# The last ten jobs of a cross network reordered, and the small tails batched to match

## The chip, the cores and the metric

The kernel runs on one core of one Trainium2 chip. The time is the device time of one execution in microseconds (us), as the median of three runs. Engines are named as the profile names them: PE is TensorE (matrix multiply), PEld its weight loads, ACT is ScalarE, DVE is VectorE, POOL is GpSimd, and SP is SyncE, which here only issues DMAs.

## The reference

A cross network of a recommender: six layers over 16384 rows of 416 features, everything in bfloat16.

```python
B, F, D, L = 16384, 26, 16, 6
Din = min(F * D, 1024)            # 416
# x0: (B, Din), ws: (L, Din, Din), bs: (L, Din)
x = x0
for l in range(L):
    proj = jnp.einsum('bd,de->be', x, ws[l]) + bs[l]
    x = x0 * proj + x
return x
```

## The kernel before, in words

**Tiles.** The rows are cut into eight groups of 2048 (four chunks of 512). Activations are held transposed: features on the 128 partitions, rows along the free axis. 416 features are three full tiles of 128 and a remainder of 32, called the tail; the tails of a group's four chunks lie side by side in the four quarters of one 128 x 512 tile. A **job** (g, l) is layer l of group g, so there are 48 jobs. A job is three output tiles of 128 features and its tail.

**One tile.** `full` (L467) issues 12 matmuls of 128x128 weights against 512 columns (three input tiles, four chunks), into four of the eight PSUM banks; `rows32` (L486) adds the contribution of the 32 tail features, with four 32-row matmuls that run side by side. `evacuate` (L378) empties the banks: ScalarE adds the bias (L406), two banks in one instruction where they are neighbours and one otherwise, VectorE multiplies by x0 (L415) and adds the old x (L420). Switching between full and 32-row matmuls is kept rare by pairing tiles: the first of a pair does full matmuls and then its rows ("FR"), the second its rows and then the full ones ("RF"). A tile without a partner ahead of a tails batch is "F1": its rows are sixteen 32x32 matmuls (L494). An FR tile's banks are all finished at its end, by the rows; an RF tile's first bank is finished when nine of the twelve full matmuls are done.

**Tails.** `tails` (L506) does the 32-feature outputs of several jobs together: 32x32 matmuls (L512), then 128x32 ones (L521), one bank for each job; `evacuate_tail` (L427) does bias (L446), multiply (L448), add (L450). For groups whose index isn't a multiple of four, the add reads a copy rotated by 32-partition steps, which two small DMAs write (`prefill` and `rotate`, L337 and L338).

**Order.** `order` (L217) lists the 48 jobs by hand: a diagonal sweep in which the jobs between two layers of one group belong to other groups. The second half mirrors the first, and L221 replaces the last six. `cuts` (L223) cuts the list into the batches of tails. `where` (L745) places each batch behind tile 0 of its second job; the last batch is placed behind tile 0 of (6, 5). L756 to 758 move tiles 1 and 2 of job (7, 4) to the end of the list. A pass behind it shifts a batch by one tile where an odd number of tiles would not stand ahead of it, and another (L797) gives each tile its mode; the last item is always "RF". The banks come from a ring of eight: four for each tile, one for each tail of a batch. The instructions are emitted in this order on each engine; a small planner derives the semaphore waits from reads and writes, and no engine's queue is reordered, SP's neither.

**When a job is done** (`done_with`, L363: three tiles and the tail) its input buffers are freed, the next rotated tail is started, and after layer 5 `output` (L687) queues on SP: DMA transposes of the three tiles into `ost` (L691) and of the tails into `ot` (L699), a copy of the tails into place (`spread`: POOL L720, for group 6 ScalarE L718), and the store (L727). For group 6 the stores are issued only ahead of the last job.

**The last job**, (7, 5), is written out by hand (from L863): it swaps the operands, so its output comes out in the layout of the result (L876: 128 rows x 416 features), and needs no transposing afterwards. For its residual, the input x of that job has to be turned into that layout: input tiles 0 and 1 by DMA (`rest_turn` L733, issue L739: tile 0 in one transpose, tile 1 in two halves), which are issued behind tiles 0 and 1 of job (7, 4); input tile 2 on TensorE (L887) and VectorE (L896); the tail on TensorE (L901) and ScalarE (L909). It starts with matmuls on input tiles 0 and 1, chunk by chunk (`nat_full`), so it needs the outputs of tiles 0 and 1 of (7, 4) at once. Each of its four rounds is then 12 matmuls of L876 with rows (L917) and bias (L922), four copies out of PSUM (L928), two multiplies (L934), two adds (L940) and a store (L947); the last round's are finer.

Of the kernel before, what the change touches and what calls it, by code (L numbers as in the profile page):

```python
# [198 lines left out]
def bass_standalone__cross_network_dcn__recsys_kernel(  # L199
# [7 lines left out]
    L = ws.shape[0]  # L207
    NT = 3
# [5 lines left out]
    LAST = NG - 1  # L214
    NX0, NXS, NX3, NTW, NTS = 5, 6, 10, 4, 4

    order = [(0, 0), (0, 1), (1, 0), (0, 2), (1, 1), (2, 0), (0, 3), (1, 2), (2, 1), (3, 0),  # L217
             (0, 4), (1, 3), (2, 2), (3, 1), (0, 5), (1, 4), (2, 3), (3, 2), (4, 0), (1, 5),
             (2, 4), (3, 3), (4, 1), (5, 0)]
    order += [(NG - 1 - g, L - 1 - l) for g, l in reversed(order)]  # L220
    order[-6:] = [(5, 5), (7, 3), (6, 4), (7, 4), (6, 5), (7, 5)]  # L221
    assert len(set(order)) == NG * L
    cuts = [1, 2, 3, 4, 4, 4, 4, 4, 4, 4, 4, 4, 3, 2]  # L223
    batches = []
    n = 0
    for c in cuts:
# [515 lines left out]
                writes=[("x5n", j, t) for j in range(j0, j1)], lane=f"x5_{t}{j0}", batch=0)  # L742

    items = []
    where = {(b[min(1, len(b) - 1)], 0): b for b in batches[:-1]}  # L745
    where[((LAST - 1, L - 1), 0)] = batches[-1]
    del where[((0, 0), 0)]
    where[((0, 1), 0)] = where.pop(((1, 0), 0))
    tiles = [((1, 0), 0), ((1, 0), 1), ((0, 1), 0), ((0, 1), 1), ((0, 1), 2), ((1, 0), 2)]
# [1 line left out]
    for jb, i in tiles:  # L751
        items.append(("tile", jb, i))
        if (jb, i) in where:
            items.append(("tails", where[(jb, i)]))

    for i in range(1, NT):  # L756
        late = items.index(("tile", (LAST, L - 2), i))
        items.append(items.pop(late))


    single = 0
# [263 lines left out]
```

## Time and profile before

| | |
|---|---|
| median of three runs | 475.86 us (475.6 to 476.08) |
| profiled execution, span | 474.40 us; its own device time is not listed, and the median less the span is 1.46 us |
| PE busy | 463.0 us of the span |
| DVE / ACT busy | 404.5 / 341.2 us |
| full matmuls L479 | 1701 recorded, 372.1 us |
| output | 13.63 MB written |

A profile line names engine, source line, operation, output<-inputs, and how many instructions are merged; a timeline line begins with start and length in us. A note in brackets tells how long the engine had been idle and for what. "SPq" lines are the issue of DMAs on SP; their data moves later. Matmul starts are recorded and their ends are modelled, so the distance between two starts is the better measure of TensorE's pace.

### The profile page before, as it was taken

The numbers are of one execution on the slowest core, as the hardware profiler recorded it, in microseconds if no ns is written. First come the engines' busy times: TensorE is split into PE (matmuls) and PEld (weight loads), VectorE is DVE, ScalarE is ACT, GpSimd is POOL, SyncE is SP. The second block draws the span as 40 slices with busy tenths as digits, with TensorE's granted clock in tenths as the row PEclk, the third lists the DMA queues.
The fourth block names the chain that finished last, engine by engine and source line by source line (L and its number), as shares of the span: only waits on it lengthen the run. The fifth ranks groups of instructions, "written<-read, shape, count | busy, mean of one in ns | idle before, by whom it ended". The sixth has DMA issues, their size and how long they took to land.

```text
span 474.4 us, 8414 instructions
## 1 busy us (share of the span) xinstructions
PE 463.0 (98%) x3354; PEld 200.0 (42%) x3408; DVE 404.5 (85%) x700; ACT 341.2 (72%) x371; POOL 6.6 (1%) x15
## 2 busy tenths in 40 slices
PE   8999999999999999999999999999999999999996
PEld 5344444654444444444444444444444444444442
DVE  1888888888888888898889869988888888888897
ACT  4687777777777777777777777777777777777775
POOL 1000000000000000000000000000000000001000
PEclk9999999999999999999999999999999999999999
DMA  8996830730102388369319950880001039026999
GB/s 224 183 176 142 177 84 1 137 87 1 33 2 46 69 234 145 76 146 233 89 24 163 245 102 7 191 271 1 1 10 27 0 62 240 22 46 102 234 166 289
DMA packets 139052, 53.18 MB, mean 112 GB/s; under 512 B 112763, under 2 KB 138501, under 8 KB 139013
## 3 DMA queue, kind: packets, MB, share of 16 engines
q1 hardware_dynamic: 138856, 52.54, 50.0%
q8 instruction: 26, 0.43, 0.4%
q10 hardware_dynamic: 156, 0.11, 0.1%
q14 instruction: 14, 0.11, 0.1%
HBM read 5.97 MB, written 13.63 MB: 41 GB/s over the span
## 4 chain that ended last, share of the span: by engine, by line
PE 92%; DMA 2%; DVE 2%; ACT 2%; issue 1%; SPq 0%; DVEq 0%
PE ps L479 77%; PE ps L500 7%; PE ps L521 6%; ACT tw L406 2%; DMA wm<-in_ws_dram 1%; PE ps L494 1%; DVE x L940 1%; DMA x<-x 1%; DVE x L934 1%; PE ps L512 1%; DMA ot<-x 1%; DVE tw L415 0%; PE ps L600 0%; SPq L545 0%; DVE x L610 0%
## 5 line engine op out<-in xcount | busy, mean ns | idle before, releaser
L406 ACT ACTIVATE tw<-ps,bias 128x1024 bf16<-128x1024 f32 (+1 forms) x295 | 299.8, 1071 | 119.5 <-PE ps L500 81.1
L479 PE MATMUL ps<-x,wm 128*128 128x512 bf16 (+1 forms) x1701 | 372.1, 371 | 6.2 <-issue 3.7
L479 PEld LDWEIGHTS ps<-x,wm 128*128 128x128 bf16 x1755 | 165.1, 98 | 209.5 <-issue 28.2
L415 DVE TENSOR_TENSOR tw<-tw,x 128x1024 bf16<-128x1024 bf16 (+1 forms) x285 | 192.6, 683 | 51.9 <-ACT tw L406 51.5
L420 DVE TENSOR_TENSOR x<-tw,x 128x1024 bf16<-128x1024 bf16 (+1 forms) x285 | 182.5, 681 | 0.0
L500 PE MATMUL ps<-x,w 32*128 32x512 bf16 x512 | 39.2, 379 | 0.0
L521 PE MATMUL ps<-x,wm 128*32 128x512 bf16 x564 | 33.0, 380 | 0.0
L446 ACT ACTIVATE ts<-ps,bias 128x512 bf16<-128x512 f32 x47 | 28.8, 701 | 0.0
L450 DVE TENSOR_TENSOR x<-ts,x 128x512 bf16<-128x512 bf16 x47 | 18.6, 417 | 3.9 <-DMA x<-x 3.9
L521 PEld LDWEIGHTS ps<-x,wm 128*32 128x32 bf16 x564 | 13.8, 96 | 17.6 <-issue 5.3
L500 PEld LDWEIGHTS ps<-x,w 32*128 32x128 bf16 x512 | 7.8, 92 | 26.9 <-issue 26.4
L448 DVE TENSOR_TENSOR ts<-ts,x 128x512 bf16<-128x512 bf16 x47 | 18.6, 418 | 0.0
L720 POOL COPY ost<-ot 128x512 bf16<-128x512 bf16 x6 | 5.1, 854 | 422.2 <-DMA ot<-x 422.2
L876 PE MATMUL ps<-wm,x 128*128 128x416 bf16 x48 | 9.7, 340 | 0.0
L610 DVE COPY x<-ps 128x512 bf16<-128x512 bf16 x5 | 2.0, 423 | 8.9 <-PE ps L600 8.9
L928 ACT ACTIVATE x<-ps 128x416 bf16<-128x416 f32 x16 | 7.7, 517 | 2.1 <-PE ps L876 1.9
L612 ACT ACTIVATE x<-ps 128x512 bf16<-128x512 bf16 x7 | 3.8, 595 | 5.6 <-PE ps L600 5.6
L876 PEld LDWEIGHTS ps<-wm,x 128*128 128x128 bf16 x48 | 4.2, 98 | 4.4 <-issue 1.0
L512 PE MATMUL ps<-x,w 32*32 32x512 bf16 x188 | 5.9, 374 | 0.0
L494 PE MATMUL ps<-x,w 32*32 32x512 bf16 x208 | 5.6, 385 | 0.0
L940 DVE TENSOR_TENSOR x<-x,x 128x832 bf16<-128x832 bf16 (+1 forms) x9 | 4.7, 541 | 0.2
L934 DVE TENSOR_TENSOR x<-x,x 128x832 bf16<-128x832 bf16 (+1 forms) x10 | 4.8, 498 | 0.0
(40 smaller groups left out, 34.0 us busy)
## 6 DMA issues: line engine op xcount, KB each, us to landing
out_dram<-ost SPq DMA_DIRECT2D x6, 1664.0 KB, 7.0
x<-x SPq DMA_DIRECT2D x24, 96.0 KB, 2.1
x<-in_x_dram SPq DMA_DIRECT2D x8, 208.0 KB, 4.9
x<-in_x_dram SPq DMA_DIRECT2D x4, 416.0 KB, 8.4
out_dram<-ost SPq DMA_DIRECT2D x2, 832.0 KB, 5.5
wm<-in_ws_dram SPq DMA_DIRECT2D x5, 312.0 KB, 3.5
x<-x SPq DMA_DIRECT2D x22, 64.0 KB, 2.0
out_dram<-x SPq DMA_DIRECT2D x3, 416.0 KB, 4.4
```

Source lines behind the costliest of these rows:

```text
L406: add("act", lambda h, a=a, w=w, b0=b0: h.activation(tw[r][:, a * CH:(a + w) * CH], psum[:, b0 * CH:(b0 + w) * CH], ACT_F.Identity, bias=b ...
L415: add("dve", lambda h, a=a, e=e: h.tensor_tensor(tw[r][:, a * CH:e * CH], tw[r][:, a * CH:e * CH], x0s[s0][:, i * GC + a * CH:i * GC + e * ...
L420: add("dve", lambda h, a=a, e=e: h.tensor_tensor(xs[so][:, i * GC + a * CH:i * GC + e * CH], tw[r][:, a * CH:e * CH], src(i, a, e), ALU.ad ...
L446: add("act", lambda h: h.activation(ts[r][:, :], bank(b), ACT_F.Identity, bias=bias[:, 3, l:l + 1], scale=1.0), reads=[("ps", b), "bias"], ...
L448: add("dve", lambda h: h.tensor_tensor(ts[r][:, :], ts[r][:, :], x03, ALU.mult), reads=[("ts", r)] + tok0, writes=[("ts", r)], release=True)
L450: add("dve", lambda h: h.tensor_tensor(x3s[so][:, :], ts[r][:, :], res, ALU.add), reads=[("ts", r)] + rtok, writes=[("x3", so), ("x3", so, ...
L479: add("pe", lambda h, t=t, j=j, k=k, w=w: h.matmul(bank(banks[j])[:, k * w:(k + 1) * w], wm[l][:, t, ecols], src(t, j, j + 1)[:, k * w:(k ...
L494: add("pe", lambda h, q=q, j=j, r=r, c=c, o=o: h.matmul(psum[o, banks[j] * CH:(banks[j] + 1) * CH], w3[l][q, i * P + c * T32:i * P + (c + ...
L500: add("pe", lambda h, q=q, j=j, r=r: h.matmul(bank(banks[j]), w3[l][q, ecols], src[q, :], start=first and not inner, stop=not first and no ...
L512: add("pe", lambda h, l=l, b=b, s3=s3, ri=ri, qi=qi, ro=ro, qo=qo: h.matmul(psum[qo, b * CH:(b + 1) * CH], w3[l][qi, NT * P:D], s3[qi, :], ...
L521: add("pe", lambda h, t=t, j=j, src=src, l=l, b=b, ro=ro, qo=qo: h.matmul(psum[qo, b * CH:(b + 1) * CH], wm[l][:, t, NT * P:D], src(t, j, ...
L876: add("pe", lambda h, t=t: h.matmul(bank(b, n=D), xcol(t, j, kk), wm[l][:, t, :], start=(first and t == 0), stop=(not first and t == NT - 1)),
```

## The change

The last ten jobs, with the tails batches that close them (each bracket is one batch):

- before: (4,5) (5,4) (6,3) (7,2) | (5,5) (7,3) (6,4) | (7,4) (6,5) | (7,5), with tiles 1 and 2 of (7,4) moved behind (6,5)
- after: (4,5) (5,4) (6,3) | (5,5) (7,2) (6,4) | (7,3) (6,5) | (7,4) | (7,5), with nothing moved

So (5,5), (6,4) and (6,5) come sooner, (7,2), (7,3) and (7,4) later; all of (6,5) lies ahead of all of (7,4). There is one batch more. From the batch that begins with (4,5) on, the items run as follows (t is a tile, T(n) a batch of n tails, tiles in brackets a pair):

- before: F1 (5,4)t0, T(4), six pairs, F1 (7,3)t1, T(3), two pairs, [(7,4)t0 (6,5)t0], F1 (6,5)t1, T(2), [(6,5)t2 (7,4)t1], (7,4)t2 alone as RF, last job
- after: F1 (5,4)t0, T(3), four pairs, F1 (7,2)t0, T(3), four pairs, F1 (6,5)t0, T(2), [(6,5)t1 (6,5)t2], F1 (7,4)t0, T(1), [(7,4)t1 (7,4)t2], last job

With that, the requests on SP's queue change places too: group 6's `output` is queued behind (6,5) and so ahead of both `rest_turn`s, where before the first `rest_turn` stood ahead of it.

```diff
-    order[-6:] = [(5, 5), (7, 3), (6, 4), (7, 4), (6, 5), (7, 5)]
+    order[-10:] = [(4, 5), (5, 4), (6, 3), (5, 5), (7, 2), (6, 4), (7, 3), (6, 5), (7, 4), (7, 5)]
     assert len(set(order)) == NG * L
-    cuts = [1, 2, 3, 4, 4, 4, 4, 4, 4, 4, 4, 4, 3, 2]
+    cuts = [1, 2, 3, 4, 4, 4, 4, 4, 4, 4, 4, 3, 3, 2, 1]
...
-    where = {(b[min(1, len(b) - 1)], 0): b for b in batches[:-1]}
-    where[((LAST - 1, L - 1), 0)] = batches[-1]
+    where = {(b[min(1, len(b) - 1)], 0): b for b in batches}
...
-    for i in range(1, NT):
-        late = items.index(("tile", (LAST, L - 2), i))
-        items.append(items.pop(late))
```

## The prediction

> **What bounds the kernel now.** I read the page's busy shares first, then the chain that ended last over its final 40 us, then the timeline of the stretch that the diff reorders (from about 383 us on), then the DMA share by stretches. From the page:
>
> ```profile
> PE 463.0 (98%) x3354; PEld 200.0 (42%) x3408; DVE 404.5 (85%) x700; ACT 341.2 (72%) x371; POOL 6.6 (1%) x15
> PEclk9999999999999999999999999999999999999999
> ```
>
> TensorE is busy for 463.0 of 474.4 us at full clock. Some 6.4 us of the idle rest lie before its first matmul and 4.5 us behind its last, so a reorder in the middle can win almost nothing: what it can do is lengthen TensorE's stream or disturb the last 20 us. TensorE's timeline around the tails:
>
> ```profile
> 382.93 0.43 PE L494 MATMUL ps<-x,w 32*32 32x512 bf16 x16
> 386.44 2.54 PE L479 MATMUL ps<-x,wm 128*128 128x512 bf16 x11 [0.16 <-issue]
> ...
> 423.89 0.43 PE L494 MATMUL ps<-x,w 32*32 32x512 bf16 x16
> 426.75 2.54 PE L479 MATMUL ps<-x,wm 128*128 128x512 bf16 x11 [0.16 <-ACT tw L406]
> 429.22 0.61 PE L500 MATMUL ps<-x,w 32*128 32x512 bf16 x8
> ```
>
> L494 is the "F1" row part ahead of a tails batch; the next L479 is the first full tile behind it. The end of the run, from the timeline of the last 40 us (the last two tiles of (7,4), then the last job at L876):
>
> ```profile
> 446.71 0.43 PE L494 MATMUL ps<-x,w 32*32 32x512 bf16 x16
> 448.92 2.54 PE L479 MATMUL ps<-x,wm 128*128 128x512 bf16 x11 [0.16 <-ACT tw L406]
> 451.39 0.61 PE L500 MATMUL ps<-x,w 32*128 32x512 bf16 x8
> 454.15 2.27 ACT L406 ACTIVATE tw<-ps,bias 128x512 bf16<-128x512 f32 x3 [0.21 <-PE ps L479]
> 454.63 0.40 PE L500 MATMUL ps<-x,w 32*128 32x512 bf16 x4
> 457.06 1.29 DVE L420 TENSOR_TENSOR x<-tw,x 128x1024 bf16<-128x1024 bf16 x2
> 457.14 0.63 ACT L718 ACTIVATE ost<-ot 128x512 bf16<-128x512 bf16 x1 [0.72 <-DMA ot<-x]
> 457.56 1.65 PE L876 MATMUL ps<-wm,x 128*128 128x416 bf16 x8
> 458.61 2.70 SPq L739 DMA_TRANSPOSE x<-x  x2
> 461.49 1.19 SPq L727 DMA_DIRECT2D out_dram<-ost  x2
> ```
>
> The reader is to see two things. L876 starts at 457.56, and its second matmul needs the half tile that L420 ends at 457.75 (457.06 + 0.68, the first of the two): TensorE hands over to the last job at the moment when VectorE is ready, with no slack. And from 455 us TensorE and VectorE are both full until 470 and 471.5 us. The chain says the same:
>
> ```profile
> 459.99 3.34 DMA x<-x
> 463.53 1.09 DVE x L940 x2
> 464.62 0.51 DVE x L934
> ```
>
> From 463.53 on VectorE runs without a gap to its end at 471.56. The DMA wait ahead of it is a tie, no stall: L934 issued at 462.51 twice would have let L940 start at 463.53 anyway.
>
> **Part 1, one more tails batch (TensorE).** From L494 to the next L479: 386.44 - 382.93 = 3.51 us for a batch of four, 2.86 of three, 2.21 of two (448.92 - 446.71). That is 0.91 + 0.65 per tail, so a batch of one takes 1.56; the trace has none in this form. Bounds: 1.34, if L521 (1.48 us for 24 matmuls, 0.76 for the 12 of the first job) sets all of it, and 2.21, a batch of two. I take 1.56, on the line of three points. Behind a batch, the first full tile takes 2.47 to its L500, and from there a pair with its rows 5.83 (435.05 - 429.22). Both plans hold 23 full tiles between 382.93 and L876:
>
> - before: 3.51 + 2.47 + 6 x 5.83; 2.86 + 2.47 + 3 x 5.83; 2.21 + 2.47 + the last two tiles 6.17 (451.39 to 457.56) = 74.63, which is 457.56 - 382.93.
> - after (batches 3, 3, 2, 1): 2.86 + 2.47 + 4 x 5.83, twice; 2.21 + 2.47 + 5.83; 1.56 + 2.47 + 3.15 = 74.99. The 3.15 is 0.55 for the rows of a pair and 2.60 for the last tile (454.96 to 457.56).
>
> **+0.36 us** on the path; nothing covers it, since TensorE is the bound there. With the bounds of the single tail: +0.14 to +1.01.
>
> The rule for it: the Trainium skill, TensorEngine Tiling (Array Packing), section Tiling Modes, says that changing the tiling mode, not just the tile, drains TensorE. That speaks against this change, which has one mode change more (32 against 31: two per pair, three per F1 with its tails, and the lone rows of the last tile fall away). A pair's 5.83 less 26 passes of 0.216 leaves 0.11 per change, so by the rule alone the loss is 0.1; the rows give more, since each batch also has its own pass of L512.
>
> **Part 2, the hand-over to the last job.** Ring positions of the last two tiles are the same (banks 7,0,1,2 and 3,4,5,6), but the tile before last, (7,4) tile 1, turns from the second of a pair (rows first) into the first (rows last). Rows-first lets ScalarE start at 454.15, when the first bank has its last matmul, 3.41 before L876. Rows-last lets it start 0.43 after L500 (L500 at 451.39, L406 at 451.82), so 3.15 - 0.43 = 2.72 before L876: **0.69 later**. Its three activations take 2.27 as before, its multiplies and adds follow, and L420's first half ends at 457.75 + 0.69 relative to the same L876. TensorE's second L876 therefore waits 0.7 us. Some comes back: the two waits for VectorE that TensorE has now in the transposes L887 (0.08 and 0.10) and one before (0.035) vanish, and 0.1 at L917 (the bank of L896). VectorE: the last tile's first multiply, now at 458.38, moves by 0.6 relative to L876, because it is queued behind that late L420; the 0.2 of waiting it has at 458.96 goes. So VectorE reaches L896 0.35 late, and the second L896, which waits for the delayed L887, about 0.48 late. From there it is full to the end. At the end 0.09 is gained: mul L934 of the last chunk waits for ScalarE now. Sum: 0.36 + 0.48 - 0.09 = 0.75, **+0.8 us in all**. Bounds of this part alone: 0 (VectorE catches up) and +0.7 (nothing comes back).
>
> **Part 3, moved DMAs.** SP's queue is in order. Now: group 5's store and rotates by 444.35, the first transpose for the last job (L739) at 445.54, group 6's transposes 447.94 to 458.57, two more L739 at 458.61 and 459.99, group 6's stores at 461.49. After: the rotates of (7,4) come behind the two tails, at about 445.9 to 447.1; group 6's transposes follow its tiles, and the first L739 comes behind them all. Issue times from the rows: 2.0 for a full transpose when DMA is free (3.1 in the busy stretch, L691), 1.2 for ot, 1.3 for a half, 1.8 for L739. Turn 0 at 447.1, turn 1 at 449.4 when its data is there, ot 452.5, halves to 456.4, L739 to 458.2. The last two L739 wait for their data anyway, the first until 458.9 (now 458.61), the second goes at 460.2; landing 3.34 later is 463.6, while VectorE would want it at 464.4. Stores at 461.7. So nothing is added, by a margin of 0.7 us on SP. ScalarE's 0.72 wait at L718 goes (ot lands by 455.0, L718 is reached at 457.5); its gain is spent on the later start of part 2: the last tile's activations start 0.2 after L876, as now.
>
> **Part 4, the other edits, at nothing.** Each job starts at least three tiles (8.7 us) after the one it depends on, and a tile's outputs are done within 4.5 us of its rows. Freed buffers: (5,5) writes the buffer that group 4's transposes free, six tiles later as (7,2) did; (6,5) writes group 5's after eight tiles, not six. The rotated tail that (7,4)'s add needs is issued by 447.1, lands in 2 to 6.7 us (L337's range) and is needed at 455.6. Odd ring positions split one activation in every second tile; pairs in that state still repeat every 5.83 us. If one of these covers fails, it costs the wait itself, some tenths to a microsecond.
>
> **Rivals.**
> 1. Forecast: +0.75, that is 476.6 (own range 476.2 to 477.0).
> 2. Part 1 only, VectorE catches up in the last job: +0.36, 476.2. For it: each of the last job's four rounds gives VectorE 2.28 us of work against 2.68 of TensorE's. Against: no gap in its timeline.
> 3. Slower on the other side of the line: SP and the transposes. If full transposes all take the 3.1 us that the busy stretch shows, SP goes 450.2, 453.3, 454.6, 457.2, L739 until 460.3, the halves until 463.0, stores at 463.1, 1.6 later. DMA decides then:
>
> ```profile
> 467.00:472.00 5.00, 2.89 (x22) 1.21 (x20) 4.46 (x11) 2.82 (x6) 0.00 (x0) 1.00 1.11 331
> 472.00:473.00 1.00, 0.00 (x0) 0.00 (x0) 0.00 (x0) 0.00 (x0) 0.00 (x0) 1.00 0.86 270
> ```
>
> The last columns are DMA share and GB/s: the engines are full until the last store. Two groups' output, 3.41 MB at 331 GB/s, is 10.3 us from 461.49 plus about 1 to start: the present end. So once the stores start more than 0.75 later than now, each further microsecond is paid in full: +1.6, 477.5; with the slowest issue seen (3.48) up to +4.
> 4. Waits were on the path: the 0.72 of L718 goes and the hand-over costs nothing: 0.36 - 0.72, 475.5.
> 5. It doesn't do what it says: group 6's last layer is sooner, but its stores stay behind the last L739 in SP's queue, so its output leaves no sooner. I hold that true; it is in the forecast.
>
> **How the numbers follow.** The page gives the span, 474.40; the runs' median is 475.86, so 1.46 lies around it. 474.40 + 0.75 + 1.46 = 476.6. A change under 0.2% (0.95 us) can't be told from none. Chances: rival 1 0.55 (0.40 within 0.2%, 0.15 over it), rival 2 0.13, rival 3 0.25, rival 4 0.07 (0.04 within, 0.03 faster). Faster 0.03, same 0.57, slower 0.40. The range leaves out the worst of rival 3 and rival 4: 475.9 to 477.8.
>
> **What would show it.** L494 to L479 of the single tail at 1.56; L876 starting at 457.9 and its second matmul a microsecond later; L718 without a wait; L739's last issue near 460.2 and the stores near 461.7; VectorE gapless from 459 to 472.3. It is wrong if TensorE shows a gap between 386 and 450, or if the stores start after 462.5.

## The result, and the profile after

The changed kernel takes 477.31 us (median of four runs, 476.59 to 477.52) where the kernel before takes 475.73 on the same chip: **1.0033 times as long, 95% interval 1.0021 to 1.0045**, or +1.58 us. That is slower by over 0.2%. The time lies in the forecast's range (475.9 to 477.8), but the forecast was 476.6, a change within 0.2%; the prediction gave slower by more than that a chance of 0.40.

In the changed kernel, code behind the edit stands five lines earlier: L876 is now L871, L934 is L929, L940 is L935, L947 is L942. From its page, busy time and the queue of instruction loads:

```profile
PE 468.1 (99%) x3420; PEld 199.7 (42%) x3420; DVE 405.0 (85%) x700; ACT 341.2 (72%) x372; POOL 6.2 (1%) x15
...
q8 instruction: 27, 0.44, 0.4%
```

Nearly all of PE's 5.1 us more than before are no work: before, the trace holds 3354 of 3408 matmuls (PEld shows how many weights were loaded). The change adds twelve, since an F1 tile has sixteen row matmuls where a pair's tile has four. The other line, 27 loads of instructions, will matter; the page of before has 26.

The span hardly tells the two apart (474.4 and 474.7), since executions differ in their first 13 us (see the end; from there to the L494 below, all ten profiles with the same stream of matmuls up to it agree to 0.01 us). So I measure from the last item that both kernels share: the rows L494 of (5,4) tile 0, at 382.93 before and 382.22 after. From there to the end of the span is 91.47 before and 92.48 after, and 91.49 and 92.48 in another profile of each. **The shared stretch is 1.01 us longer.** All times called "rel." count from this L494. All engines' timeline of after, from the single tail on:

```profile
450.03 0.43 PE L494 MATMUL ps<-x,w 32*32 32x512 bf16 x16
...
451.37 2.76 PE L479 MATMUL ps<-x,wm 128*128 128x512 bf16 x12
...
454.07 0.61 PE L500 MATMUL ps<-x,w 32*128 32x512 bf16 x8
454.49 2.27 ACT L406 ACTIVATE tw<-ps,bias 128x512 bf16<-128x512 f32 x3 [1.28 <-PE ps L500]
...
455.59 5.17 SPq L739 DMA_TRANSPOSE x<-x  x3
456.64 0.64 ACT L718 ACTIVATE ost<-ot 128x512 bf16<-128x512 bf16 x1
457.21 0.34 PE L871 MATMUL ps<-wm,x 128*128 128x416 bf16 x1
457.40 1.29 DVE L420 TENSOR_TENSOR x<-tw,x 128x1024 bf16<-128x1024 bf16 x2
458.15 1.41 PE L871 MATMUL ps<-wm,x 128*128 128x416 bf16 x7 [0.60 <-DVE x L420]
460.94 1.14 SPq L727 DMA_DIRECT2D out_dram<-ost  x2
```

The reader is to see four things. The single tail costs 1.34 from L494 to L479. ScalarE's L406 starts 2.72 ahead of the last job (457.21), where it started 3.41 ahead before. So the last job's second matmul comes 0.94 behind its first and waits for VectorE's L420. And L718 has no wait any more, and group 6's stores leave at 460.94, which is rel. 78.72 against 78.56 before. The end of the chain of waits:

```profile
457.49 1.20 DVE x L420 x2
...
463.64 1.09 DVE x L935 x2
...
471.09 0.28 DVE x L935
```

The DMA wait that stood in the chain of before (the last transpose) is gone: it runs through L420 into VectorE's work. Its last add starts 0.79 later (rel. 89.06 against 88.27) and takes 0.37, as before. But the span ends 1.01 later; the rest is behind VectorE. The last stretches (length, busy time of each engine, granted clock, DMA share, GB/s):

```profile
467.00:472.00 5.00, 2.98 (x22) 1.21 (x20) 4.55 (x11) 2.91 (x6) 0.00 (x0) 1.00 0.97 297
472.00:473.00 1.00, 0.00 (x0) 0.00 (x0) 0.00 (x0) 0.00 (x0) 0.00 (x0) 1.00 0.75 247
473.00:474.00 1.00, 0.00 (x0) 0.00 (x0) 0.00 (x0) 0.00 (x0) 0.00 (x0) 1.00 0.05 13
```

The share of 0.05 at the end is one engine of sixteen still at work while fifteen have stopped: from rel. 90.81 to 91.42 the trace has packets of 832 bytes one behind the other only.

### The profile page after: what moved, and what is told of

Its sections match the earlier page's. It is cut to its first block, busy times and chain, and to the rows that moved or that the text cites. A ratio compares the mean times of both kernels' runs of the same rounds, so it can differ in the third digit from the quotient of the medians.

```text
span 474.7 us, 8497 instructions
## 1 busy us (share of the span) xinstructions
PE 468.1 (99%) x3420; PEld 199.7 (42%) x3420; DVE 405.0 (85%) x700; ACT 341.2 (72%) x372; POOL 6.2 (1%) x15
## 4 chain that ended last, share of the span: by engine, by line
PE 95%; DVE 3%; ACT 1%; issue 0%; DVEq 0%
PE ps L479 78%; PE ps L500 7%; PE ps L521 7%; PE ps L494 1%; DVE x L935 1%; DVE x L929 1%; PE ps L512 1%; PE ps L600 1%; PE ps L582 1%; DVE x L420 0%; ACT tw L406 0%; DVE tw L415 0%; ACT x L612 0%; DVE x L891 0%; PE ps L620 0%
## 5 line engine op out<-in xcount | busy, mean ns | idle before, releaser
L406 ACT ACTIVATE tw<-ps,bias 128x1024 bf16<-128x1024 f32 (+1 forms) x296 | 299.9, 1069 | 120.5 <-PE ps L500 80.1
L479 PE MATMUL ps<-x,wm 128*128 128x512 bf16 (+1 forms) x1755 | 379.6, 372 | 0.5 <-ACT x L612 0.5
L479 PEld LDWEIGHTS ps<-x,wm 128*128 128x128 bf16 x1755 | 164.9, 98 | 209.5 <-issue 29.2
L420 DVE TENSOR_TENSOR x<-tw,x 128x1024 bf16<-128x1024 bf16 (+1 forms) x285 | 183.0, 683 | 0.0
L871 PE MATMUL ps<-wm,x 128*128 128x416 bf16 x48 | 9.8, 340 | 0.6 <-DVE x L420 0.6
L871 PEld LDWEIGHTS ps<-wm,x 128*128 128x128 bf16 x48 | 4.2, 98 | 5.1 <-issue 1.4
L494 PE MATMUL ps<-x,w 32*32 32x512 bf16 x224 | 6.1, 385 | 0.0
L929 DVE TENSOR_TENSOR x<-x,x 128x832 bf16<-128x832 bf16 (+1 forms) x10 | 4.9, 499 | 0.0
L935 DVE TENSOR_TENSOR x<-x,x 128x832 bf16<-128x832 bf16 (+1 forms) x9 | 4.7, 541 | 0.2
```

Of the source, the lines that this page charges most:

```text
L406: add("act", lambda h, a=a, w=w, b0=b0: h.activation(tw[r][:, a * CH:(a + w) * CH], psum[:, b0 * CH:(b0 + w) * CH], ACT_F.Identity, bias=b ...
L420: add("dve", lambda h, a=a, e=e: h.tensor_tensor(xs[so][:, i * GC + a * CH:i * GC + e * CH], tw[r][:, a * CH:e * CH], src(i, a, e), ALU.ad ...
L479: add("pe", lambda h, t=t, j=j, k=k, w=w: h.matmul(bank(banks[j])[:, k * w:(k + 1) * w], wm[l][:, t, ecols], src(t, j, j + 1)[:, k * w:(k ...
L494: add("pe", lambda h, q=q, j=j, r=r, c=c, o=o: h.matmul(psum[o, banks[j] * CH:(banks[j] + 1) * CH], w3[l][q, i * P + c * T32:i * P + (c + ...
L871: add("pe", lambda h, t=t: h.matmul(bank(b, n=D), xcol(t, j, kk), wm[l][:, t, :], start=(first and t == 0), stop=(not first and t == NT - 1)),
```

## The experiments

What each left, from its profile. "Last job" is its first matmul, "wait" the distance to its second; "15 of 16" is when fifteen of the sixteen DMA engines have landed their part of the last store, "lag" how long the sixteenth takes after that. The end follows the last landing by 0.47 to 0.49. All rel., in us; a ratio is of median times, with its 95% interval. VectorE's last add is told by its start, here and in the expectations; it takes 0.37 everywhere.

| kernel | last job | wait | first store issued | last add starts | 15 of 16 | lag | end | loads | time ratio |
|---|---|---|---|---|---|---|---|---|---|
| before | 74.63 | 0.24 | 78.56 | 88.27 | 90.61 | 0.37 | 91.47 | 26 | |
| after | 74.99 | 0.94 | 78.72 | 89.06 | 91.20 | 0.81 | 92.48 | 27 | 1.0033 [1.0021, 1.0045] |
| after_again | 74.99 | 0.94 | 78.70 | 89.06 | 91.19 | 0.82 | 92.48 | 27 | 1.0028 [1.0018, 1.0039] |
| before_again | 74.63 | 0.25 | 78.59 | 88.26 | 90.66 | 0.35 | 91.49 | 26 | 0.9999 [0.9991, 1.0008] |
| order_alone | 74.63 | 0.25 | 79.20 | 88.13 | 91.18 | 0.34 | 91.99 | 26 | 1.0016 [1.0007, 1.0024] |
| handover_alone | 74.67 | 0.99 | 78.46 | 88.80 | 90.93 | 0.80 | 92.22 | 27 | 1.0024 [1.0015, 1.0033] |
| split_alone | 75.18 | 0.25 | 78.94 | 88.59 | 90.95 | 0.35 | 91.78 | 26 | 1.0008 [1.0000, 1.0017] |
| tile_major | 74.99 | 0.18 | 78.77 | 88.95 | 91.18 | 0.96 | 92.62 | 27 | 1.0030 [1.0019, 1.0041] |
| add_first | 74.99 | 0.18 | 78.81 | 88.81 | 91.11 | 1.02 | 92.62 | 27 | 1.0030 [1.0019, 1.0042] |
| order_short | 74.63 | 0.25 | 79.33 | 88.26 | 90.39 | 0.01 | 90.89 | 26 | 0.9992 [0.9983, 1.0001] |
| after_fewer | 74.99 | 0.93 | 79.43 | 89.06 | 91.45 | 0.38 | 92.31 | 26 | 1.0017 [1.0006, 1.0027] |
| handover_fewer | 74.67 | 0.99 | 78.53 | 88.79 | 90.93 | 0.01 | 91.42 | 26 | 1.0005 [0.9997, 1.0014] |
| add_first_fewer | 74.99 | 0.18 | 79.26 | 88.80 | 91.28 | 0.38 | 92.15 | 26 | 1.0018 [1.0009, 1.0027] |
| before_more | 74.63 | 0.24 | 78.17 | 88.01 | 90.14 | 0.37 | 91.00 | 26 | 1.0006 [0.9998, 1.0015] |

The theory I started with (A) was that the tails batch and VectorE's late hand-over make the loss; the rivals were that the stores' place in SP's queue makes it, or the order itself.

### The change taken apart

**after_again**: the changed kernel once more, for the scale of the others.

> The changed kernel once more. In the two profiles the stretch from the rows L494 of job (5,4) tile 0 (the last item that both kernels share) to VectorE's last add is 0.80 us longer after the change (89.07 against 88.27 us), while the medians differ by 1.58 us. Theory A: 0.8 us is all that the change costs; the rest is where the runs happened to start (the first matmul with weights starts at 6.55 us in the profile of before and at 5.84 in that of after). Then new runs give a difference near 0.8 us, +0.6 to +1.1. Rival B: the change costs 1.5 us, part of it outside the profiled stretch; then +1.4 to +1.7 again.

+1.41 us by the medians (476.85 against 475.44), which is rival B's number, and the stretch came out the same to 0.01 us. So the stretch does not hold all of the difference in time; it repeats much better than the time, and later differences are read from it.

**order_alone**: the new order with the old batches of tails, so that batches and hand-over stay as before.

Against the changed kernel:

```diff
-    cuts = [1, 2, 3, 4, 4, 4, 4, 4, 4, 4, 4, 3, 3, 2, 1]
+    cuts = [1, 2, 3, 4, 4, 4, 4, 4, 4, 4, 4]
...
+    where[((5, 4), 0)] = [(4, 5), (5, 4), (6, 3), (7, 2)]
+    where[((6, 4), 1)] = [(5, 5), (7, 3), (6, 4)]
+    where[((6, 5), 2)] = [(7, 4), (6, 5)]
```

> The new order of the jobs, with the old batches of four, three and two tails, so as many batches as before, and the last tile again alone with its rows first. Theory A (the batches and the hand-over cost, the order itself nothing): the shared stretch is 88.3 us, as before the change, and the time is within 0.3 us of before. Rival B (the order, or the DMA requests that it moves on SP's queue, costs): +0.5 us or more stays.

Theory A's limit of 0.3 us did not hold: the time grew by 0.68. The end is 0.52 later, though VectorE is done 0.14 sooner: what is late is the stores, by 0.64. SP's part of the timeline shows it:

```profile
456.51 5.11 SPq L739 DMA_TRANSPOSE x<-x  x3
461.80 1.13 SPq L727 DMA_DIRECT2D out_dram<-ost  x2
```

SP's queue is in order, and these stand behind the transposes of group 6. Here the last batch, with (6,5)'s tail, stands behind (6,5)'s third tile and not its first, so the tails' transpose L699 is issued at rel. 69.89 (after: 68.87), and all that is queued behind it is late. That comes from where I put the batch; so the run shows what late stores cost, with TensorE and VectorE as before or better, and not what the order costs by itself.

**handover_alone**: the old order, with the tile before last made the first of a pair, and so the one ahead of it an F1, which brings the same twelve matmuls as the change.

```diff
     mode[len(items) - 1] = "RF"
+    mode[len(items) - 2] = "FR"
+    mode[len(items) - 3] = "F1"
```

> The old order and the old batches; only the pairing of the last three tiles is changed, so that the last two are a pair, as after the change: the tile before last has its rows last. Theory A (the hand-over to the last job): TensorE gets to the last job at the same distance within 0.1 us, but the second matmul of it waits some 0.7 us longer for VectorE, of which 0.45 us is left at the end: +0.45 us. Rival C (VectorE catches up in the last job): the wait is there, and +0.1 us or less at the end.

The wait grew from 0.24 to 0.99 and the last add came 0.53 later, but the end 0.75 later, although the stores left 0.10 sooner. More was lost behind VectorE than in it: the first sign that a term was missing.

**split_alone**: the old order, with the tail of (7,2) in a batch of its own.

```diff
+    whole = next(it[1] for it in items if it[0] == "tails" and (7, 2) in it[1])
+    whole.remove((7, 2))
+    items.insert(items.index(("tile", (7, 2), 0)) + 1, ("tails", [(7, 2)]))
```

> The old order and the old end; only the tail of (7,2) is taken out of its batch of four and done in a batch of its own, behind (7,2) tile 0, between two pairs. Theory A (one more batch lengthens TensorE's stream): +0.35 to +0.45 us, all of it on the path, visible as the distance to the first matmul of the last job. Rival D (a small batch hides in TensorE's stream, the loss is all hand-over): +0.1 us or less.

One more batch costs TensorE 0.55 here (75.18 less 74.63), more than the 0.35 to 0.45 expected, the last add 0.32 and the end 0.31; the time grew by 0.40 us, with an interval that begins at no change. The loss is there in the stretch, and 0.23 of it is taken up between TensorE and VectorE's last add.

### Does the hand-over set the end?

**before_again**: the kernel before, against itself.

> The kernel before, unchanged, timed against itself: what two runs of one program can differ by. Theory A: ratio 1.000 within 0.0008, and in its profile the stretch from the rows L494 of (5,4) tile 0 to VectorE's last add is 88.27 us again, to the end of the span 91.47 us, each within 0.1. Rival B (the profiled execution of before was a slow one): the stretch to the end is 0.3 us or more shorter, and the change costs that much more than the 1.01 us that the two profiles show there.

The comparison tells differences from about 0.1% on.

**tile_major** takes TensorE's wait away: the last job's first eight matmuls go by input tile, so that the four on tile 1 come after the four on tile 0.

```diff
-    for j in range(NJ):
-        nat_full(0, j, bks[0][j], True, (0, 1))
+    for j, t in [(j, t) for t in (0, 1) for j in range(NJ)]:
+        nat_full(0, j, bks[0][j], True, (t,))
```

> The changed kernel, with the first eight matmuls of the last job in another order: all four of input tile 0 first, then the four of input tile 1. TensorE's second matmul then needs nothing late; its first use of (7,4) tile 1 comes 0.5 us later. Theory A1 (the price of the hand-over is VectorE's late queue, TensorE's wait is only its sign): TensorE's wait of 0.70 us shrinks to 0.2, and it waits again at the transposes of input tile 2; the end moves by 0 to -0.1 us. Theory A2 (the price is TensorE's wait itself): -0.4 to -0.5 us.

**add_first** makes VectorE sooner: for (7,4) tile 1 it adds the first half before it multiplies the second.

```diff
-                writes=[("x", so, i, k) for k in rng], hold=True)
+                writes=[("x", so, i, k) for k in rng], hold=(g, l, i) != (LAST, L - 2, 1))
```

> The changed kernel, with one change on VectorE: for tile 1 of (7,4) it adds the first half before it multiplies the second. The first half is then ready 0.9 us sooner, in the gap where VectorE waits for ScalarE, the second half 0.15 to 0.4 us sooner. Theory A (the hand-over costs): TensorE's 0.70 us wait at the second matmul of the last job goes to under 0.1, VectorE's last add comes 0.2 to 0.4 us sooner, and the time falls by 0.2 to 0.5 us. Rival E (the end is set by the drain of the stores alone): the last add moves, the end doesn't (within 0.1 us).

Both took the wait from 0.94 to 0.18 and the last add forward, by 0.11 and 0.25. The end didn't follow: it came 0.14 later, and the times are those of the changed kernel: neither A2's gain of 0.4 to 0.5 nor the 0.2 to 0.5 expected of add_first is there. **With that theory A falls as an account of the end**: VectorE's lateness is real, but 0.25 us less of it is worth nothing here.

**order_short** leaves out group 6's second store, to see whether the DMA engines set the end.

Against order_alone:

```diff
-    store(LAST - 1, 2, NJ)
```

> The new order with the old batches, as in order_alone, and the second of group 6's two stores left out (rows 13312 to 14335 of the result are not written). In order_alone VectorE's last add came 0.14 us sooner than before the change and the end 0.52 later, with the stores issued 0.64 later. Theory F (the DMA engines are full from the first of these stores to the end, so the end follows the stores): 0.85 MB less to write, and the end is 0.4 to 0.6 us sooner than in order_alone, only as far as VectorE's last store lets it. Rival G (the last store's own latency sets the end): within 0.1 us of order_alone.

It takes 1.10 off order_alone's end with the last add 0.13 later, more than the 0.4 to 0.6 expected. So in order_alone the stores set the end. With one store less, fifteen engines have landed 2.13 after the start of the last add, the smallest distance in the table (2.13 or 2.14 in five other rows): there the end hangs on VectorE.

### The load of instructions

In after, after_again, handover_alone, tile_major and add_first, the trace has a 27th load of instructions on queue q8, 16 KB on one DMA engine for 0.88 us, at rel. 85.2 to 85.9: in the middle of the last stores. No other kernel has it. In those five one engine lands its part of the last store 0.80 to 1.02 after the other fifteen; in before, order_alone and split_alone 0.34 to 0.37. To take it away without touching the end, I made the stream of instructions shorter far ahead of it: `halves` (L465) is the number of full matmuls of jobs (1,2), (2,1) and (3,0) that are issued as two halves, so 47 for 63 gives sixteen fewer matmuls.

```diff
-    halves = [63]
+    halves = [47]
```

**handover_fewer**, **after_fewer** and **add_first_fewer** are handover_alone, after and add_first with that edit.

> handover_alone (old order and batches, the last two tiles a pair) with the 16 matmuls fewer. Theory H: what is left is the hand-over itself. VectorE's last add stays at 88.80 us (0.53 over before), the lag of the one engine goes from 0.80 to 0.4, the end comes at 91.75 to 91.9 us instead of 92.22: +0.3 to +0.4 us over before instead of +0.75. Rival I: 92.2 again.

> In the profiles of the changed kernel, and of handover_alone, tile_major and add_first, a load of instructions of 16 KB (a 27th; before the change, in order_alone and split_alone there are 26) runs on one of the 16 DMA engines for 0.88 us in the middle of the last stores, and that engine's part of every later store lands 0.8 to 1.1 us behind the other 15 (0.35 before the change). This is the changed kernel with 16 matmuls fewer in its instruction stream, long before the reordered jobs: 47 instead of 63 full matmuls of the first groups are issued as two halves. Theory H (the added row matmuls push the stream over one more load, and the load delays the end): 26 loads, the lag back at 0.4, VectorE's last add as in the changed kernel (89.06 us after the shared L494, within 0.1), the end of the span at 92.0 to 92.1 us instead of 92.48, and the time 0.4 us below the changed kernel's. Rival I (the lag comes from how the stores fall together, not from the load): the end stays at 92.4 to 92.5.

> add_first (the changed kernel, VectorE adds the first half of (7,4) tile 1 before it multiplies the second) with the 16 matmuls fewer. In add_first VectorE's last add came 0.25 us sooner than in the changed kernel and the end 0.14 later, which spoke for a drain that sets the end alone. Theory H: without the load the gain shows: last add 88.8 us, end 91.8 to 92.0, that is 0.1 to 0.2 us below after_fewer and 0.5 to 0.7 below the changed kernel. Rival E: the end of after_fewer again, within 0.05.

handover_fewer is the clean pair. Last job, wait and last add are as in handover_alone to 0.01, the first store is issued 0.07 later, the other fifteen engines land at 90.93 in both, and only the sixteenth differs: lag 0.80 with the load, 0.01 without. The landings show that the load adds a late engine: at the last job's second store, behind the load, two engines of handover_alone are behind the other fourteen, by 0.44 and 1.41, and in handover_fewer one is behind, by 0.44. Some engine lags by 0.3 to 0.4 without the load too (see the table); what makes that smaller lag was not tried. The end falls by 0.80 and the time by 0.84 us; what is left, +0.2 us, can't be told from no change. From the two profiles' DMA views of 460 to 475 us (issues with KB and median us to landing), with the load (handover_alone):

```profile
q8 instruction: 1, 0.02, 0.4%
...
out_dram<-x SPq DMA_DIRECT2D x3, 416.0 KB, 4.7
out_dram<-x SPq DMA_DIRECT2D x1, 208.0 KB, 3.1
out_dram<-x SPq DMA_DIRECT2D x1, 104.0 KB, 2.5
```

and without (handover_fewer), where this view has no q8 line:

```profile
out_dram<-x SPq DMA_DIRECT2D x3, 416.0 KB, 3.8
out_dram<-x SPq DMA_DIRECT2D x1, 208.0 KB, 2.2
out_dram<-x SPq DMA_DIRECT2D x1, 104.0 KB, 1.7
```

The reader is to see that every store behind the load lands 0.8 to 0.9 later, the last like the first: that one engine does not catch up ahead of the end.

In after_fewer the lag fell too (0.81 to 0.38), but the stores were issued 0.71 later, so the end gained only 0.17 of the 0.4 to 0.5 expected. There the 26th load lies in the transposes at rel. 70.97 for 1.16 us (in after at 70.51, for 0.88), the L691 issued at 70.31 takes 2.31 on SP (in after 1.63), and the last L739 lands 0.75 later. It seems that the load was moved to a place that costs as well; the time is 0.46 us shorter than after_again's. add_first_fewer ends 0.16 sooner than after_fewer, within the 0.1 to 0.2 expected, but later than the 91.8 to 92.0 named, and its stores were issued 0.17 sooner too, so this doesn't show that VectorE's 0.26 was what helped.

**before_more** is the test from the other side: the kernel before with `halves = [79]`, meant to bring the load about there.

> The kernel before, with 16 matmuls more in its instruction stream, at the same early place: 79 full matmuls are issued as two halves instead of 63; nothing else is changed. Theory H: a 27th load falls into the last stores, one DMA engine lands 1.0 to 1.2 us behind the others, VectorE's last add stays at 88.27 us, and the end moves from 91.48 to 92.1 or 92.3: +0.6 to +0.9 us without any change of the order. Rival I: no change of the end beyond 0.1 us.

No 27th load came. The expectation failed by its size: the three jobs hold only 72 matmuls that may be halved, so the edit added nine and not sixteen. The end moved even so, and the other way, to 91.00. SP's queue there, with the transposes of group 6 and its stores:

```profile
444.83 1.73 SPq L739 DMA_TRANSPOSE x<-x  x1
447.24 6.17 SPq L691 DMA_TRANSPOSE ost<-x  x2
453.47 1.26 SPq L699 DMA_TRANSPOSE ot<-x  x1
...
460.39 1.14 SPq L727 DMA_DIRECT2D out_dram<-ost  x2
```

The L494 is at 382.22 here. The 26th load comes at rel. 67.37 for 0.99 us, before at 69.20 for 1.37; the second L691 then takes 2.70 on SP instead of 3.12, the stores leave 0.39 sooner, VectorE's last add starts 0.26 sooner and the end is 0.47 sooner. So nine matmuls far ahead, with the order as before, move the end of the stretch by half of what the change costs there, and the likely cause, argued and not isolated, is again the place of a load. The time did not follow (+0.19 us, interval -0.1 to +0.7). Counting TensorE's weight loads (one for each matmul) that had begun when each load started gives:

```
kernel                     weight loads   25th load at   26th load at   27th load at
after_fewer                        3404           3142           3282              -
handover_fewer                     3404           3151           3277              -
before                             3408           3148           3282              -
split_alone                        3408           3147           3280              -
before_more                        3417           3157           3278              -
handover_alone                     3420           3148           3290           3408
after                              3420           3153           3296           3410
add_first                          3420           3153           3296           3413
```

The last loads come at nearly the same places of TensorE's stream in all kernels (within 20 weight loads), on average some 130 apart, and only the streams of 3420 have one more. All fourteen profiles agree with a limit between 3417 and 3420. That it is the length of TensorE's stream that decides, and no other engine's, is argued from this. The runs with 16 matmuls fewer show that the last pair alone does not bring the load; that the twelve matmuls would bring it without that pair was to be shown by before_more, and is not shown.

## Why the prediction was right or wrong

**Part 1** held: +0.36 on TensorE was predicted, and the last job starts at 74.99 against 74.63. Two errors cancel in it. The single tail costs 1.34, the lower bound, and not 1.56; the first tile behind a batch takes 2.70 and not 2.47. Both errors are one: a matmul of 0.22 whose record is missing before ("x11" in the lines of before, "x12" now), so that each batch seemed that much longer and the tile behind it that much shorter. The sum held because of that. On the rule of the Trainium skill, TensorEngine Tiling (Array Packing), Tiling Modes: by the drain alone the sum was 0.1, and the rows' 0.36 was measured.

**Part 2** held as a mechanism to a tenth and less: the wait is 0.94 (predicted 0.24 + 0.7), ScalarE starts 2.72 ahead (2.72), VectorE's last add is 0.79 later (0.75 with Part 1).

**Part 3** held: L718 lost its wait, and the stores left at 460.94, at rel. 78.72 (predicted 461.7, which is 78.77). Its doubt, rival 3, is borne out in order_alone and order_short: where the stores start late, DMA decides. But 0.64 of lateness cost 0.52 there with VectorE on time, so the stores had no margin of their own; rival 3's 0.75 holds only beside a VectorE that is late by as much.

**Part 4** held: TensorE has no gap between 382 and 457; pairs repeat every 5.83.

**What failed** is the last step, "Sum: 0.36 + 0.48 - 0.09 = 0.75", taken as the end of the run. It has two faults:

1. VectorE's lateness isn't paid in full. In handover_fewer the last add is 0.52 later and the end 0.05 sooner. Before, the end lay 0.2 to 0.6 behind what the last add alone asks for: fifteen engines landed 2.34 after its start, and the sixteenth 0.37 later still; in handover_fewer it is 2.14 and 0.01. Of the 0.52, fifteen engines paid 0.32, and the lag that is gone gave back 0.36. DMA was the bound already, and VectorE had that much slack.
2. A term is missing: with the twelve more row matmuls of the additional F1 tile comes a 27th load of instructions, among the last stores. The prediction counted their time and not that they have to be loaded.

For after this gives: fifteen engines land 0.59 later (91.20 less 90.61), with the last add 0.79 later, and the sixteenth lags 0.44 more. Together 1.03, the stretch's 1.01. Without the load the lag would be between 0.01 (handover_fewer) and 0.38 (after_fewer), and so the end 0.2 to 0.6 later than before, an estimate from these rows; the load is the other 0.4 to 0.8. No run shows that split for the changed kernel directly, since in after_fewer the stores left later as well. That the time still lies in the range is in part luck: the load was in no term of it, and its upper end, 477.8, was drawn for late stores.

A smaller fault: the working took 1.46 for what lies around a span. In the profiled executions whose own time is known it is 1.8 to 1.9 (476.59 less 474.7 for after, 476.27 less 474.5 for before_again). So the profiled execution of before, with its 474.40, was one of the longer ones; its L494, at 382.93, is the second latest of the fourteen.

**What stays open.** The profiles show +1.01, the medians of timed runs +1.41 and +1.58. Their intervals, 0.9 to 1.9 and 1.0 to 2.1, just reach the former; in all the other kernels with an edit too the time grew 0.1 to 0.7 us more than the stretch. If the stretch is as constant in every execution as in the two profiles of each kernel, the rest lies ahead of it, in the first 13 us; no run shows that, and I don't know its cause. Nor was it tried whether ten or eleven more matmuls bring the load.

No kernel here beats the one before by more than the measurement can tell.

## What to carry to other kernels

Where stores run to the last microsecond, follow the slowest of the sixteen DMA engines and not the last engine that computes: an earlier VectorE gains only what the stores don't hold back. A handful of added instructions can cost more than their own time (here 0.8 us at the end of handover_alone), if one more load of instructions falls into a stretch in which the DMA engines are full; compare the count and the places of these loads in both traces, and shorten the stream somewhere else if one fell badly. And measure a late change from the last item that both kernels share, so that the start's variation drops out.

## What the runs showed of the hardware

- A load of instructions is 16 KB on one DMA engine: 0.88 us with stores beside it, up to 1.7 elsewhere. It put that engine about 1 us behind the rest, and it was still 0.80 or more behind at the last of the six stores that landed after it.
- With sixteen engines busy, the two stores of group 6 and those of the last job, 4096 packets of 832 bytes, took 10.8 us from first packet to last in seven profiles without such a load (10.74 to 10.85), and 11.7 in five with it (11.68 to 11.76). In handover_fewer, without it, they took 11.00; VectorE is late there, and the DMA share falls to 0.85 in the 2 us from rel. 86.0 on (before: 1.12).
- Executions differ at the start although the code is the same there. The first L479 stands at 6.55 in the timeline of before:

```profile
6.55 1.46 PE L479 MATMUL ps<-x,wm 128*128 128x512 bf16 x6 [0.53 <-DMA wm<-in_ws_dram]
```

and at 5.84 in that of after, the releaser another:

```profile
5.84 1.46 PE L479 MATMUL ps<-x,wm 128*128 128x512 bf16 x6 [0.51 <-ACT x L612]
```

Over all profiles the shared stretch began between 381.91 and 382.98. So 0.7 us of the difference between two spans can come from here alone: it hides most of this change's loss.
